# Decode attention with a 16,384-long cache: the weighted sum of V with V as the moving operand in four column groups

## The chip, the cores and the metric

One core of a Trainium2 chip. The metric is device time in microseconds (us), lower is better. A program of one core has no second die to compare with; runs count as undisturbed ("fast") by the rule that a run must lie within 1.5% of the fastest of its kernel.

## The reference, cut to what matters

```python
# B, H, Sk, Dh, D = 2, 32, 16384, 128, 1024; bf16 throughout
def _A_ref(x, k_cache, v_cache, wq, wo):              # attention of one new token
    q = (x @ wq).reshape(B, 1, H, Dh).transpose(0, 2, 1, 3)
    scores = einsum("bhqd,bhkd->bhqk", q, k_cache) * Dh ** -0.5
    p = softmax(scores)
    o = einsum("bhqk,bhkd->bhqd", p, v_cache)         # <- the change is here
    return o.transpose(0, 2, 1, 3).reshape(B, 1, H * Dh) @ wo
# ... _B_ref: a small mixer block on its own weights (about 18.9 MB)
out = g * _A_ref(...) + (1 - g) * _B_ref(...)         # g: a sigmoid gate
```

There are 64 pairs of batch and head. Each has 4 MB of K and 4 MB of V, read once and used for one query. All loads together are 572.5 MB.

## The kernel before

K and V tiles share a ring of five 4 MB buffers (128 partitions x 32 KB). One queue (SP) issues all the big loads, in the order K of pair i+1, V of pair i, and each load waits for the buffer used five loads earlier. Partition p holds rows 128p to 128p+127 of the cache; `V[:, j, :]` is the 128 x 128 slice of row j of every partition.

```python
NM = 8; CJ = NJ // NM                       # NJ = 128 rows per partition, CJ = 16
def qk_stage(i):                            # scores of a pair
    for m in range(NM):
        nc.vector.transpose(out=T..., in_=Kw[:, m * CW : (m + 1) * CW]...)   # 32x32 blocks
        for v in range(4):
            nc.tensor.matmul(S[:], lhsT=z[:, v, 7 - m : 7 - m + P],
                             rhs=Tb[:, v // 2, :, v % 2], start=..., stop=...)   # 512 columns
# softmax_stage: max, exp on ACT, PT = the exponentials, transposed in 32x32 blocks
def pv_stage(i):                            # weighted sum of V
    tot_ps = misc_psum([P, 1], FP32)
    nc.tensor.matmul(tot_ps[:], lhsT=quarter_f[:], rhs=rs[:], start=True, stop=True)
    nc.vector.reciprocal(out=rinv[:], in_=tot_ps[:])
    oc = ops.tile([P, 1], FP32, name="oc")
    for j in range(NJ):                     # 128 weight loads of V, 128 one-column matmuls
        nc.tensor.matmul(oc[:], lhsT=V[:, j, :], rhs=PT[:, j % CJ, j // CJ : j // CJ + 1],
                         start=(j == 0), stop=(j == NJ - 1))
    nc.vector.tensor_scalar(out=OT[:, h, b : b + 1], in0=oc[:], scalar1=rinv[:, 0:1], ...)
# [cut: q projection, gate, mixer, output projection]
```

## Time and profile before

| | before |
|---|---|
| time, median | 1355.92 us |
| span of the profiled run | 1353.7 us, 24,547 instructions |
| DMA share, 40 to 1280 us | 1.00, at 429 GB/s |
| PE busy | 971.3 us (72%) |
| weighted sum of a pair on PE | 3.3 to 3.5 us, 256 instructions |

The page of the kernel before: instructions, busy times, then the DMA queues (packets, MB, share of the time of 16 DMA engines). q1 is the queue of the loads; q8 and q14 bring instructions.

```profile
span 1353.7 us, 24547 instructions
PE 971.3 (72%) x11260; PEld 525.9 (39%) x11260; DVE 752.0 (56%) x948; ACT 51.7 (4%) x132; POOL 34.0 (3%) x79
...
q1 hardware_dynamic: 24628, 572.54, 98.8%
q8 instruction: 88, 1.44, 0.4%
q14 instruction: 15, 0.12, 0.0%
```

The table by stretches (us, busy time of each engine, PE clock, DMA share, GB/s) of the same kernel, for the middle:

```profile
40.00:600.00 560.00, 417.36 (x4680) 228.13 (x4679) 319.37 (x402) 21.38 (x56) 13.51 (x28) 0.72 1.00 429
600.00:1280.00 680.00, 488.32 (x5541) 257.31 (x5539) 382.09 (x467) 25.69 (x66) 16.26 (x34) 0.74 1.00 429
```

```profile
1326.00:1330.00 4.00, 0.65 (x2) 0.25 (x3) 1.95 (x2) 0.00 (x0) 0.00 (x0) 0.50 0.99 418
1333.00:1337.00 4.00, 4.00 (x15) 1.54 (x14) 3.54 (x4) 0.00 (x0) 0.00 (x0) 0.79 0.55 236
1342.00:1346.00 4.00, 4.00 (x141) 4.00 (x139) 1.10 (x3) 0.15 (x2) 0.00 (x0) 0.50 0.52 211
```

In the middle all 16 DMA engines are busy all the time. From 1333 to 1346 us only 0.55, then 0.52 of the DMA engines' time is used. If every load is dealt out evenly over the 16 engines, as its 128 packets of 32 KB suggest (8 for each engine), some engines have fallen behind during the run.

Two groups of the kernel before (line, engine, operation, out<-in, count, busy us, mean ns, then idle time just before and what ended it):

```profile
L247 DVE STREAM_TRANSPOSE T<-Kn 128x1024 f32<-128x1024 f32 x512 | 597.0, 1217 | 202.7 <-DMA Kn<-in_A_k_cache_dram 174.7
...
L296 PE MATMUL oc<-PT,Vn 128*128 128x1 bf16 x8192 | 221.5, 164 | 0.7 <-issue 0.7
```

The vector engine waits 174.7 us for K: compute has slack. The weighted sum is the second line.

### The profile page before, as it was taken

The page shows a single profiled execution, that of the slowest core. Times are in us where ns is not written, and L with a number is a line of the kernel's source. Part 1 is how long each engine was busy: PE and PEld are TensorE (multiplying, and loading weights), DVE is VectorE, ACT ScalarE, POOL GpSimd, SP SyncE. Part 2 cuts the span into 40 slices and gives each one's busy share as a digit, 9 for nine tenths or more (in the row PEclk, how much of TensorE's full clock was granted, in tenths as well). Part 3 has the DMA queues.
Part 4 walks back from the last instruction along what each step waited for, and adds up shares of the span by engine and source line. Part 5 has one row for each costly group of instructions (what it writes and reads, how often), then busy time and mean ns, then how long its engine had stood idle before and what let it go on. Part 6 is the DMA issues. An engine that isn't in the chain of part 4 may idle for free.

```text
span 1353.7 us, 24547 instructions
## 1 busy us (share of the span) xinstructions
PE 971.3 (72%) x11260; PEld 525.9 (39%) x11260; DVE 752.0 (56%) x948; ACT 51.7 (4%) x132; POOL 34.0 (3%) x79
## 2 busy tenths in 40 slices
PE   2787677787777777677676767767766776776767
PEld 2343343344444344343433334334333333333434
DVE  2766555565545654556545555655655664665564
ACT  0000000000000000000000000000000000000000
POOL 0000000000000000000000000000000000000000
PEclk9887676766767766777676868777767777867876
DMA  9999999999999999999999999999999999999995
GB/s 403 431 434 425 429 431 428 430 430 428 430 429 428 430 429 430 432 427 428 431 430 428 431 427 433 426 430 433 427 428 431 426 434 430 427 427 431 427 433 242
DMA packets 25011, 574.11 MB, mean 424 GB/s; under 512 B 3014, under 2 KB 3014, under 8 KB 7372
## 3 DMA queue, kind: packets, MB, share of 16 engines
q1 hardware_dynamic: 24628, 572.54, 98.8%
q8 instruction: 88, 1.44, 0.4%
q14 instruction: 15, 0.12, 0.0%
q10 hardware_dynamic: 280, 0.01, 0.0%
HBM read 572.53 MB, written 0.00 MB: 423 GB/s over the span
## 4 chain that ended last, share of the span: by engine, by line
DMA 70%; PE 20%; DVE 6%; issue 2%; ACT 1%; DVEq 0%; POOL 0%; ACTq 0%
DMA Kn<-in_A_k_cache_dram 69%; PE S L255 12%; PE oc L296 5%; DVE T L247 5%; DMA x_pm<-in_A_x_dram 2%; DVE m L266 1%; PE misc L400 1%; PE misc L272 1%; PE misc L199 1%; ACT Pr L277 1%; PE misc L373 1%; DVE mx L270 0%; PE misc L268 0%; PE misc L291 0%; DVE nb L274 0%
## 5 line engine op out<-in xcount | busy, mean ns | idle before, releaser
L247 DVE STREAM_TRANSPOSE T<-Kn 128x1024 f32<-128x1024 f32 x512 | 597.0, 1217 | 202.7 <-DMA Kn<-in_A_k_cache_dram 174.7
L255 PE MATMUL S<-T,z_131 128*128 128x512 bf16 x704 | 211.0, 464 | 82.3 <-DVE T L247 81.8
L255 PE MATMUL S<-T,z_135 128*128 128x512 bf16 x672 | 201.5, 464 | 83.9 <-DVE T L247 83.5
L255 PE MATMUL S<-T,z_133 128*128 128x512 bf16 x672 | 201.3, 463 | 75.7 <-DVE T L247 75.2
L296 PE MATMUL oc<-PT,Vn 128*128 128x1 bf16 x8192 | 221.5, 164 | 0.7 <-issue 0.7
L296 PEld LDWEIGHTS <-Vn 128*128 128x128 bf16 x8192 | 220.8, 100 | 1.4 <-issue 0.8
L255 PEld LDWEIGHTS <-z_131 128*128 128x128 bf16 x704 | 79.0, 112 | 215.0 <-issue 162.5
L255 PEld LDWEIGHTS <-z_135 128*128 128x128 bf16 x672 | 75.1, 112 | 210.3 <-issue 160.7
L255 PEld LDWEIGHTS <-z_133 128*128 128x128 bf16 x672 | 75.3, 112 | 201.6 <-issue 152.0
L303 DVE TENSOR_SCALAR OT<-oc,rinv 128x1 bf16<-128x1 f32 x64 | 14.2, 221 | 150.6 <-PE oc L296 150.6
L277 ACT ACTIVATE Pr<-S,nb 128x512 bf16<-128x512 f32 x64 | 44.0, 687 | 1236.4 <-DVE nb L274 1211.8
L266 DVE TENSOR_REDUCE m<-S 128x1 f32<-128x512 f32 x64 | 44.3, 692 | 76.2 <-PE S L255 76.2
L281 DVE STREAM_TRANSPOSE PT<-Pr 128x512 bf16<-128x512 bf16 x64 | 45.5, 711 | 56.4 <-ACT Pr L277 56.4
L291 PE MATMUL misc<-rs,quarter_f 128*128 128x1 f32 x128 | 31.9, 318 | 35.8 <-ACT Pr L277 35.8
L268 PE MATMUL misc<-ident_f,m 128*1 128x128 f32 x64 | 17.7, 276 | 45.4 <-DVE m L266 45.4
L272 PE MATMUL misc<-mx,nscale_f 1*128 1x1 f32 x128 | 25.0, 262 | 24.6 <-DVE mx L270 24.6
L291 PEld LDWEIGHTS misc<-rs,quarter_f 128*128 128x128 f32 x128 | 27.1, 264 | 38.6 <-ACT Pr L277 38.6
L268 PEld LDWEIGHTS misc<-ident_f,m 128*1 128x1 f32 x64 | 5.2, 81 | 76.1 <-DVE m L266 75.2
L272 PEld LDWEIGHTS misc<-mx,nscale_f 1*128 1x128 f32 x128 | 19.5, 190 | 37.3 <-DVE mx L270 37.3
L270 DVE TENSOR_REDUCE mx<-misc 1x1 f32<-1x128 f32 x64 | 17.8, 278 | 26.8 <-PE misc L268 26.6
L274 DVE COPY nb<-misc 128x1 f32<-128x1 f32 x64 | 10.0, 157 | 30.0 <-PE misc L272 30.0
L225 POOL TENSOR_TENSOR z_131<-qsel,own 128x64 bf16<-128x64 bf16 x22 | 10.5, 477 | 429.5 <-PE S L255 423.0
(77 smaller groups left out, 184.4 us busy)
## 6 DMA issues: line engine op xcount, KB each, us to landing
Kn<-in_A_k_cache_dram SPq DMA_DIRECT2D x64, 4096.0 KB, 42.7
Vn<-in_A_v_cache_dram SPq DMA_DIRECT2D x63, 4096.0 KB, 39.9
wt<-in_B_w_dram SPq DMA_DIRECT2D x4, 3584.0 KB
woh<-in_A_wo_dram SPq DMA_DIRECT2D x32, 256.0 KB, 39.7
wq_156<-in_A_wq_dram SPq DMA_DIRECT2D x1, 4096.0 KB, 12.2
wq_158<-in_A_wq_dram SPq DMA_DIRECT2D x1, 4096.0 KB, 21.7
wt<-in_B_w_dram SPq DMA_DIRECT2D x2, 2048.0 KB
Vn<-in_A_v_cache_dram SPq DMA_DIRECT2D x1, 2048.0 KB
```

The source lines that it names most:

```text
L199: nc.tensor.matmul(qps[:, h, :], lhsT=wq_half[half][:, r, h * Dh : (h + 1) * Dh], rhs=xT[:, half * rn + r, :], start=(r == 0), stop=(r == ...
L247: nc.vector.transpose(out=T[:].rearrange("p w j s -> p j w s"), in_=Kw[:, m * CW : (m + 1) * CW].rearrange("p (j w e) -> p j w e", w=2, e=32),
L255: nc.tensor.matmul(S[:], lhsT=z[:, v, 7 - m : 7 - m + P], rhs=Tb[:, v // 2, :, v % 2], start=(m == 0 and v == 0), stop=(m == NM - 1 and v ...
L266: nc.vector.reduce_max(out=m[:], in_=S[:], axis=AX.X)
L268: nc.tensor.transpose(mT[:], m[:], ident_f[:])
L270: nc.vector.reduce_max(out=mx[:], in_=mT[:], axis=AX.X)
L272: nc.tensor.matmul(nb_ps[:], lhsT=nscale_f[:], rhs=mx[:], start=True, stop=True)
L277: nc.scalar.activation(out=Pr[:], in_=S[:], func=ACTF.Exp, bias=nb[:], scale=scale, accum_out=rs[:])
L281: nc.vector.transpose(out=PT[:].rearrange("p j m -> p (j m)"), in_=Pr[:])
L291: nc.tensor.matmul(tot_ps[:], lhsT=quarter_f[:], rhs=rs[:], start=True, stop=True)
L296: nc.tensor.matmul(oc[:], lhsT=V[:, j, :], rhs=PT[:, j % CJ, j // CJ : j // CJ + 1], start=(j == 0), stop=(j == NJ - 1),)
L303: nc.vector.tensor_scalar(out=OT[:, h, b : b + 1], in0=oc[:], scalar1=rinv[:, 0:1], scalar2=None, op0=ALU.mult)
```

## The change

Its intent: V becomes the moving operand. One matmul streams four rows of V (512 columns) past 32 columns of weights, and four such matmuls, in four 32-column groups of the PE array, are to run side by side. That leaves a 128 x 512 block of which only some rows of some columns matter; it is copied out of PSUM and four products with a constant selection matrix pick and sum them. The last pair keeps the old form, as its V arrives last and the new form has a longer way from the last byte to the result.

```diff
+    osel = const.tile([P, 4], FP32)
+    nc.vector.tensor_copy(out=osel[:], in_=ident_f[:, 0:8:2])
+    for g in range(1, 4):
+        nc.vector.tensor_tensor(
+            out=osel[:], in0=osel[:], in1=ident_f[:, 40 * g : 40 * g + 8 : 2], op=ALU.add)
...
+    def pv_rows(V, PT, oc):
+        O = ops.tile([P, 4 * Dh], FP32, name="O")
+        for m in range(NM):
+            lhsT = PT[:].rearrange("p j m -> p (j m)")[:, m : CJ * 32 : 16]
+            for g in range(4):
+                j0 = m * CJ + 4 * g
+                nc.tensor.matmul(O[32 * g : 32 * g + 32, :], lhsT=lhsT, rhs=V[:, j0 : j0 + 4, :],
+                                 start=(m == 0), stop=(m == NM - 1))
+        Os = rows.tile([P, 4, Dh], FP32, name="Os")
+        nc.scalar.copy(out=Os[:].rearrange("p x d -> p (x d)"), in_=O[:])
+        for x in range(4):
+            nc.tensor.matmul(oc[:], lhsT=Os[:, x, :], rhs=osel[:, x : x + 1],
+                             start=(x == 0), stop=(x == 3))
+    def pv_cols(V, PT, oc):                 # the old loop
...
-        oc = ops.tile([P, 1], FP32, name="oc")
-        for j in range(NJ): ...
+        oc = misc_psum([P, 1], FP32)
+        (pv_rows if i < NPAIR - 1 else pv_cols)(V, PT, oc)
```

To free a PSUM bank, the result column moves into three shared PSUM buffers, and the last product of the mixer no longer holds two of these between its halves: each half is summed and added by itself (cut here).

More of the change, by code (lines that the diff above doesn't have):

```diff
@@ L157 @@
         nc.vector.memset(own[32 * a : 32 * a + 32, 4 * a : 4 * a + 4], 1.0)
+    assert CJ == 16
+    osel = const.tile([P, 4], FP32)
+    nc.vector.tensor_copy(out=osel[:], in_=ident_f[:, 0:8:2])
+    for g in range(1, 4):
+        nc.vector.tensor_tensor(
+            out=osel[:], in0=osel[:], in1=ident_f[:, 40 * g : 40 * g + 8 : 2], op=ALU.add
+        )
     ZW = P + 8
@@ L283, in softmax_stage @@
         rs_tiles[i] = rs
+    def pv_rows(V, PT, oc):
[4 more added lines that the diff above has]
+                j0 = m * CJ + 4 * g
+                nc.tensor.matmul(
+                    O[32 * g : 32 * g + 32, :],
+                    lhsT=lhsT,
+                    rhs=V[:, j0 : j0 + 4, :],
+                    start=(m == 0),
+                    stop=(m == NM - 1),
+                )
+        Os = rows.tile([P, 4, Dh], FP32, name="Os")
+        nc.scalar.copy(out=Os[:].rearrange("p x d -> p (x d)"), in_=O[:])
+        for x in range(4):
+            nc.tensor.matmul(
+                oc[:], lhsT=Os[:, x, :], rhs=osel[:, x : x + 1], start=(x == 0), stop=(x == 3)
+            )
+    def pv_cols(V, PT, oc):
+        for j in range(NJ):
+            nc.tensor.matmul(
+                oc[:],
+                lhsT=V[:, j, :],
+                rhs=PT[:, j % CJ, j // CJ : j // CJ + 1],
+                start=(j == 0),
+                stop=(j == NJ - 1),
+            )
     def pv_stage(i):
@@ L293, in pv_stage @@
         nc.vector.reciprocal(out=rinv[:], in_=tot_ps[:])
-        oc = ops.tile([P, 1], FP32, name="oc")
-        for j in range(NJ):
-            nc.tensor.matmul(
-                oc[:],
-                lhsT=V[:, j, :],
-                rhs=PT[:, j % CJ, j // CJ : j // CJ + 1],
-                start=(j == 0),
-                stop=(j == NJ - 1),
-            )
+        oc = misc_psum([P, 1], FP32)
+        (pv_rows if i < NPAIR - 1 else pv_cols)(V, PT, oc)
         nc.vector.tensor_scalar(
@@ L394 @@
     wt = {}
-    b_ps = []
     def linear_rows(w, actT, r0, rn, dst, first, last):
@@ L439, in st_lin4 @@
     def st_lin4(half):
-        if half == 0:
-            b_ps.extend(misc_psum([B, W], FP32) for _ in range(DH2))
-        linear_rows(wt.pop(f"w4{half}"), h2T, half * (FC // 2), FC // 2, b_ps, half == 0, half == 1)
+        ps = [misc_psum([B, W], FP32) for _ in range(DH2)]
+        linear_rows(wt.pop(f"w4{half}"), h2T, half * (FC // 2), FC // 2, ps, True, True)
+        for n in range(DH2):
+            sl = slice(n * W, (n + 1) * W)
+            nc.vector.tensor_tensor(
+                out=pre_row[:, sl], in0=(x1_row if half == 0 else pre_row)[:, sl], in1=ps[n][:], op=ALU.add
+            )
         if half == 1:
-            for n in range(DH2):
-                sl = slice(n * W, (n + 1) * W)
-                nc.vector.tensor_tensor(out=pre_row[:, sl], in0=x1_row[:, sl], in1=b_ps[n][:], op=ALU.add)
             nc.vector.tensor_scalar(
```

## The prediction

> **What bounds it now.** The loads. The queue table gives the SP queue 98.8% of the time of 16 DMA engines over a 1353.7 us span (572.5 MB, mean 424 GB/s). The table by stretches shows a DMA share of 1.00 at 429 GB/s from 40 to 1280 us: the transfers never wait for a buffer. The ring of five 4 MB tiles is refilled 40 to 43 us ahead (issue table, time to landing). The chain of waits is 70% DMA. The Trainium skill ("DMA: Bandwidth & Descriptors", Specifications) gives a fabric ceiling of 435 GB/s; the trace's 429 agrees that little is left.
>
> A pair of K and V (8.39 MB) takes 19.6 us at 429 GB/s. Compute has slack: in the list of waits the vector engine waits for K 174.7 us in 60 times (2.9 us a pair).
>
> **What the change does,** per pair, for 63 of 64:
> - Removes 128 one-column matmuls with 128 weight loads of V: 3.3 to 3.5 us in the timeline, 27 ns each (221.5 us in all).
> - Adds 32 matmuls of 512 columns. In the trace a 512-column score matmul follows the last by 0.43 us at the low clock, 0.22 at the high. Estimates: four column groups side by side, 8 x 0.22 to 0.43 = 1.8 to 3.4 us; one after another, 7 us (14 at the low clock). The skill ("TensorE: Matmul & The Clock Gate", Packing small matmuls) reports 2.38x for three column tiles; I expect about 3x for four: 2.3 to 4.6 us.
> - Adds a 128x512 ACT copy, about 0.69 us (as the 128x512 exponential), and four fp32 selection matmuls, 0.3 to 0.5 us each by the fp32 sum with `quarter_f` (two passes, 0.38 to 0.57 us): 1.2 to 2 us, plus about 1 us of handoffs.
>
> So a pair's weighted sum goes from 3.5 us to about 5 (4 to 8). The added 1.5 us fits in the 2.9 us of slack and the 30 us of prefetch. Little of the change lies on the critical path.
>
> Two small terms remain. The instruction queue moved 1.44 MB; with some 11,000 of 24,547 instructions fewer 0.65 MB goes, 1.5 us at 429 GB/s (an estimate). At the end the last V lands at about 1348.3 us and 5 us of work follow, unchanged; the pair before it is off that path by about 0.7 us, so its selection may add 0 to 1 us.
>
> **Predicted: 1354.8 us, 8 in 10 between 1352.0 and 1362.0. Faster by over 2%: 1%; within 2%: 93%; slower by over 2%: 6%.**
>
> **What would show each step right.** DMA share still 1.00 at 428 to 431 GB/s in the middle; instruction bytes near 0.8 MB; the 32 matmuls of a pair done in 2 to 4.6 us; the vector engine's wait for K shorter by about 1.5 us a pair, yet not zero; chain still led by the K loads; last V landing within 3 us of before.
>
> **What would make it wrong.** If the column groups run one after another, the stage takes 7 us at the high clock plus 3 for copy and selection: 6 us over, more than the slack; then K waits for compute, DMA share drops under 0.97 and the time is 1380 to 1480. Waits might also come from the single buffers of the new tiles, or the 3 shared PSUM buffers that now also hold the result column. If the transfers share something with PE's reads of V, the rate in the middle would change (430 to 433 GB/s would give 5 to 10 us); I expect no change. Faster by 2% would need a rate above 437 GB/s.

## The result, and the profile after

The time fell from 1355.92 us (four runs, 1355.86 to 1356.09) to 1347.86 us (four runs, 1347.82 to 1348.12). The ratio is 0.9941, 95% interval 0.9924 to 0.9958. Ratios are the mean time of one kernel's fast runs over that of the other's of the same rounds, so not quite the ratio of the medians. The change is within 2%, as forecast, but 8.1 us is more than the range allowed: it lies below its lower end of 1352.

The page after, in the same order:

```profile
span 1346.0 us, 13528 instructions
PE 955.1 (71%) x5716; PEld 452.2 (34%) x5716; DVE 743.6 (55%) x954; ACT 88.4 (7%) x195; POOL 34.4 (3%) x79
...
q1 hardware_dynamic: 24628, 572.54, 99.3%
q8 instruction: 44, 0.72, 0.2%
q14 instruction: 15, 0.12, 0.0%
```

The stretches after, middle and end (1338 to 1340 us in place of 1326 to 1330, as the end comes sooner):

```profile
40.00:600.00 560.00, 411.04 (x2429) 197.33 (x2427) 315.65 (x403) 36.61 (x83) 14.13 (x29) 0.75 1.00 430
600.00:1280.00 680.00, 485.06 (x2644) 222.16 (x2645) 378.99 (x472) 46.18 (x102) 16.05 (x33) 0.76 1.00 430
```

```profile
1333.00:1337.00 4.00, 2.04 (x19) 1.40 (x11) 0.57 (x3) 1.20 (x3) 0.00 (x0) 0.84 0.56 232
1338.00:1340.00 2.00, 2.00 (x77) 2.00 (x77) 0.01 (x1) 0.00 (x0) 0.00 (x0) 0.50 0.38 143
1342.00:1346.00 4.00, 0.84 (x2) 0.00 (x0) 1.40 (x2) 0.00 (x0) 0.00 (x0) 0.50 0.00 1
```

PE busy time hardly moved, and the bytes loaded are the same. What halved is the q8 queue: 88 packets of 16 KB became 44. And the lopsided end is shorter: nine engines still work at 1333 us as before, but at 1342 the loads are over, where before eight engines had 5 us to go.

The new stage in the timeline of a pair (start us, length us):

```profile
1312.70 1.96 PE L302 MATMUL O<-Vn,PT 128*32 128x512 bf16 x32
...
1314.77 0.58 ACT L310 COPY Os<-O 128x512 f32<-128x512 f32 x1 [16.64 <-PE O L302]
...
1315.40 1.05 PE L312 MATMUL misc<-osel,Os 128*128 128x1 f32 x8 [0.74 <-ACT Os L310]
```

All 32 matmuls take 1.96 us, the copy 0.58, the selection 1.05: with the handoffs 3.8 us, against 3.5. Single records show four matmuls starting 2 to 5 ns after one another, and the next four 207 ns after the last of them: the four groups do run side by side. The Trainium skill ("TensorE: Matmul & The Clock Gate", Packing small matmuls) gives about 4 ns per tile; this trace agrees.

And the vector engine's wait for K:

```profile
L255 DVE STREAM_TRANSPOSE T<-Kn 128x1024 f32<-128x1024 f32 x512 | 596.1, 1216 | 114.7 <-DMA Kn<-in_A_k_cache_dram 89.9
```

It fell from 174.7 to 89.9 us, 1.3 us a pair. That is the loss of slack that was forecast, and the DMA share of 1.00 in the middle shows that it is harmless.

One more thing changes, at the very end. The last pair's K, and after the change its products with V (128 weight loads and matmuls, as before), in the timelines before and after:

```profile
1328.05 4.62 DVE L247 STREAM_TRANSPOSE T<-Kn 128x1024 f32<-128x1024 f32 x4 [2.81 <-DMA Kn<-in_A_k_cache_dram]
```

```profile
1337.96 3.55 PE L318 MATMUL misc<-PT,Vn 128*128 128x1 bf16 x128 [0.16 <-DVE PT L289]
```

Before, the vector engine starts on the last K at 1328.05 us, after at 1320.86: also 7.2 us sooner. Before, PE stands still for 0.73 us before the last 29 of the products, about when the last piece of V lands. After, the products run without a gap, so there the path to the end leads from the landing of the last K and not from the last V. Both landings wait for the engines that are late.

### When each DMA engine ends

The trace does not number the engines, but its packet records let one see when an engine runs dry: a packet end that no packet start follows within 60 ns, where each start is counted for one end only. Worked out so, to within some tenths of a microsecond, the last load packets end at:

```
                q8 packets   early group        one between   late group
before          88           7, 1330.8-1332.1   1340.5        8, 1347.4-1347.7
after           44           7, 1330.6-1332.2   } 1338.6-1338.8 and 1340.0-1340.5, about half each
```

So eight engines are 16 us late before, and 7 to 9 us late after. 88 packets over 8 engines are 11 each; 44 are 5.5, that is 5 on some and 6 on others, and the late group has indeed split in two, 1.5 us apart. 11 x 1.46 = 16.1 us, 6 x 1.46 = 8.8, 5 x 1.46 = 7.3. The factor 1.46 is this lag divided by these counts. Packet times give nearly the same: an instruction packet itself takes 1.07 us (mean of 88), and the load packet right behind it some 1.7 us in place of 1.22: about 1.5 us for both.

**Theory.** PE's instructions are fetched over 8 of the 16 DMA engines, 256 at a time (22,520 in 88 packets). Each fetch makes its engine about 1.5 us late with the loads. The engines share each load evenly, so the engine with the most fetches sets when the last loads, of K and of V, are complete. The change halves PE's instructions and with them this lag; that V moves is not what counts.

**Rivals.** (a) Reading V as weights took something from the transfers into the same memory. (b) The new stage frees buffers sooner, or does better work on PE. (c) One of the side parts (PSUM, mixer) did it.

### The profile page after: what moved, and what is told of

Its sections match the earlier page's. It is cut to its first block, busy times and chain, and to the rows that moved or that the text cites. A ratio compares the mean times of both kernels' runs of the same rounds, so it can differ in the third digit from the quotient of the medians.

```text
span 1346.0 us, 13528 instructions
## 1 busy us (share of the span) xinstructions
PE 955.1 (71%) x5716; PEld 452.2 (34%) x5716; DVE 743.6 (55%) x954; ACT 88.4 (7%) x195; POOL 34.4 (3%) x79
## 4 chain that ended last, share of the span: by engine, by line
DMA 61%; PE 26%; DVE 8%; issue 2%; ACT 1%; DVEq 0%; POOL 0%; ACTq 0%
DMA Kn<-in_A_k_cache_dram 37%; DMA Vn<-in_A_v_cache_dram 22%; PE S L263 14%; DVE T L255 6%; PE O L302 5%; PE misc L433 2%; DMA x_pm<-in_A_x_dram 2%; PE misc L312 2%; PE misc L407 1%; ACT Pr L285 1%; DVE PT L289 1%; ACT Os L310 1%; PE misc L207 1%; PE misc L280 0%; PE misc L318 0%
## 5 line engine op out<-in xcount | busy, mean ns | idle before, releaser
L255 DVE STREAM_TRANSPOSE T<-Kn 128x1024 f32<-128x1024 f32 x512 | 596.1, 1216 | 114.7 <-DMA Kn<-in_A_k_cache_dram 89.9
L302 PE MATMUL O<-Vn,PT 128*32 128x512 bf16 x2016 | 133.3, 410 | 40.0 <-DMA Vn<-in_A_v_cache_dram 40.0
L337 DVE TENSOR_SCALAR OT<-misc,rinv 128x1 bf16<-128x1 f32 x64 | 14.1, 221 | 246.1 <-PE misc L312 242.6
L263 PEld LDWEIGHTS <-z_136 128*128 128x128 bf16 x704 | 81.7, 116 | 180.3 <-issue 125.7
L263 PEld LDWEIGHTS <-z_138 128*128 128x128 bf16 x672 | 78.7, 117 | 183.5 <-issue 132.7
L263 PEld LDWEIGHTS <-z_140 128*128 128x128 bf16 x672 | 79.3, 118 | 176.4 <-issue 126.4
L302 PEld LDWEIGHTS <-PT 128*32 128x32 bf16 x2016 | 69.9, 143 | 100.5 <-DMA Vn<-in_A_v_cache_dram 48.0
L312 PE MATMUL misc<-osel,Os 128*128 128x1 f32 x504 | 69.6, 259 | 47.2 <-ACT Os L310 47.2
L310 ACT COPY Os<-O 128x512 f32<-128x512 f32 x63 | 36.9, 585 | 994.5 <-PE O L302 994.5
L312 PEld LDWEIGHTS misc<-osel,Os 128*128 128x128 f32 x504 | 64.2, 200 | 78.4 <-ACT Os L310 78.4
L332 PE MATMUL misc<-rs,quarter_f 128*128 128x1 f32 x128 | 35.8, 349 | 67.0 <-ACT Pr L285 67.0
L332 PEld LDWEIGHTS misc<-rs,quarter_f 128*128 128x128 f32 x128 | 30.7, 297 | 72.7 <-ACT Pr L285 72.3
## 6 DMA issues: line engine op xcount, KB each, us to landing
Kn<-in_A_k_cache_dram SPq DMA_DIRECT2D x64, 4096.0 KB, 46.1
```

The costliest lines, as they stand in the source:

```text
L255: nc.vector.transpose(out=T[:].rearrange("p w j s -> p j w s"), in_=Kw[:, m * CW : (m + 1) * CW].rearrange("p (j w e) -> p j w e", w=2, e=32),
L263: nc.tensor.matmul(S[:], lhsT=z[:, v, 7 - m : 7 - m + P], rhs=Tb[:, v // 2, :, v % 2], start=(m == 0 and v == 0), stop=(m == NM - 1 and v ...
L302: nc.tensor.matmul(O[32 * g : 32 * g + 32, :], lhsT=lhsT, rhs=V[:, j0 : j0 + 4, :], start=(m == 0), stop=(m == NM - 1),)
L310: nc.scalar.copy(out=Os[:].rearrange("p x d -> p (x d)"), in_=O[:])
L312: nc.tensor.matmul(oc[:], lhsT=Os[:, x, :], rhs=osel[:, x : x + 1], start=(x == 0), stop=(x == 3))
```

## The experiments

All runs: correct against the reference unless said, beside the kernel before on the same chip (1355.95 to 1356.06 us). A caution: a kernel that was wrong passed the comparison too (`const` below), so "correct" says little about the weighted sum here.

### ctrl: everything but the moving V

```diff
-        (pv_rows if i < NPAIR - 1 else pv_cols)(V, PT, oc)
+        pv_cols(V, PT, oc)
```

> The changed kernel with V stationary for all 64 pairs; every other part of the change stays (selection constant, result column in the shared PSUM buffers, the last product of the mixer summed in two parts). Fetch theory (instruction fetches ride on 8 of the 16 DMA engines, delay their loads by about 1.5 us each, and the slowest engine sets the end): the instruction count is back at about 24,500, so 88 instruction packets and 1356 us (1354.5 to 1357.5). If the side parts made the gain: 1348.

Measured: 1355.34 us (1354.59 to 1356.04), ratio 0.9995 (0.998 to 1.001), 88 instruction packets, late engines at about 1347.8 (one at 1346.1). Rival (c) falls: the side parts give about half a microsecond.

### const: the same instructions, V not read as weights

```diff
-                lhsT=V[:, j, :],
+                lhsT=V[:, 0, :] if j == 0 else ident_bf[:],
```

> The kernel before with the same 128 weight loads and matmuls a pair, but 127 of the 128 weight loads read the constant identity in place of V (wrong result on purpose; the first still reads V, so that the buffer is held until then). Fetch theory: same instructions, so 88 packets and 1355.9 us, within 1 us. Rival (reading V into the array as weights takes something from the transfers that write the same memory): with these reads gone the time falls to 1350 or below, the rate in the middle rises.

Measured: 1355.90 us (1355.64 to 1356.30), ratio 1.000, 88 packets, late engines at 1347.4 to 1347.6 but for one that ends sooner, the middle still at 429 GB/s. Rival (a) falls: 127 of 128 reads of V less, and nothing gained.

### pad_pe and pad_pool: two pads that did not test what they should

```diff
 # pad_pe, in pv_stage
+        for _ in range(96 if i < NPAIR - 1 else 0):
+            nc.tensor.ldweights(ident_bf[:, 0:32])
 # pad_pool, in build_z
+        for _ in range(192):
+            nc.gpsimd.nop(nofuse=True)
```

> The changed kernel plus 96 weight loads of a constant (32 columns) a pair on PE, 6,048 instructions in all, without any other work. Fetch theory: 24 instruction packets more (44 to 68), 24 / 8 x 1.45 us = 4.3 us later: 1352.2 us (1350.5 to 1354), and the two groups of DMA engines finish about 12.5 us apart instead of 8. Rivals (reads of V, or buffers freed sooner): 1347.9, unless the 1 to 3 us of PE time a pair make compute the bound; that would show as a DMA share under 1.00 in the middle.

> The changed kernel plus 192 empty instructions a pair on POOL, about 12,300 in all, where nothing waits for them. Fetch theory, if fetches of every engine use the same DMA engines: 48 packets more (44 to 92), 48 / 8 x 1.45 = 8.7 us later: 1356.6 us (1354 to 1359). If POOL's fetches use other DMA engines than PE's, they load the early ones and the time stays near 1348 to 1350. Rivals: 1347.9 in any case, since PE, V and the buffers are as in the changed kernel.

Measured: pad_pe 1483.50 us (1482.92 to 1484.33). The constant depends on no pair, so all 6,048 weight loads were scheduled to the front, where the loads stood still for some 130 us (2 GB/s in three slices of the page). It had 68 instruction packets, but the late engines end at 1474.2 to 1476.1 against 1466.4 to 1468.0 for the early: 8 us apart as with 44. The 24 extra packets were fetched at the front (the pad runs from 1.5 us to about 180), most of them while the load queue was idle. That fits the theory (a fetch costs only where it displaces a load), though it was not the test.

pad_pool: 1347.85 us (1347.63 to 1348.95), 44 packets, no instruction more in the trace. The empty instructions left no mark on either instruction queue, so the run says nothing about the theory. Both pads missed what was expected of them (1352.2 and 1356.6 us).

### pad48 and pad96: the change with PE instructions given back

The pads now read the pair's own weights, so they stay in their place:

```diff
+        for _ in range(48 if i < NPAIR - 1 else 0):      # pad96: 96
+            nc.tensor.ldweights(PT[:, 0, :])
         oc = misc_psum([P, 1], FP32)
```

> The changed kernel plus 48 idle weight loads (of the pair's own weights, so that they stay in their place) a pair on PE: 3,024 instructions, 12 packets more, 56 in all. Fetch theory in its sharper form (the packets go round 8 DMA engines, each delays its engine by 1.46 us, the engine with most of them ends last): 7 on each in place of 5 or 6, so the last load lands 1.5 us later, at about 1341.7, and the time is 1349.3 us (1348.3 to 1350.3). Rivals (V as weights; PE work in itself): 1347.9, or later only with a DMA share under 1.00 in the middle.

> The same with 96: 6,048 instructions, 68 packets. Fetch theory: 8 or 9 on each of 8 engines, the last load lands at 1331.5 + 9 x 1.46 = 1344.6, 4.4 us later than in the changed kernel: 1352.2 us (1351 to 1353.5), if compute with 2 us more of PE a pair still keeps up (DMA share 1.00 in the middle). Rivals: 1347.9.

Measured: pad48 1349.08 us (1348.66 to 1349.29), pad96 1352.38 us (1352.02 to 1352.81), against 1349.3 and 1352.2 expected. The queue lines of both pages, pad48 first:

```profile
q8 instruction: 56, 0.92, 0.3%
```

```profile
q8 instruction: 68, 1.11, 0.3%
```

The late engines end at 1341.7 to 1341.9 in pad48 (56 packets, 7 each: the group is one again), and in pad96 (68, or 8.5 each) in two groups, 1343.0 to 1343.2 and 1344.8 to 1344.9. The stretches of pad96, middle and end:

```profile
600.00:1280.00 680.00, 482.19 (x2691) 304.62 (x5857) 384.00 (x474) 45.62 (x100) 16.58 (x34) 0.78 1.00 430
```

```profile
1338.00:1340.00 2.00, 1.33 (x10) 1.13 (x10) 0.41 (x2) 0.24 (x1) 0.00 (x0) 0.93 0.53 223
1342.00:1346.00 4.00, 3.63 (x129) 3.48 (x128) 0.46 (x3) 0.00 (x0) 0.00 (x0) 0.50 0.23 89
```

The middle is untouched (share 1.00), so compute keeps up and only the end moves. Over all runs with even flow (not `pad_pe`, `g_outer` and the two `rebal` runs, whose loads stood still or slowed down) the end of a late engine against its number of packets is:

```
packets on the engine    5        6        7        8        9        11
last load ends, us       1338.7   1340.3   1341.8   1343.1   1344.8   1347.6
```

(1347.6 - 1338.7) / 6 = 1.48 us a packet. This is the test that rival (b) fails: V moves and PE does the same useful work as in the changed kernel, yet 4.5 of the 8.1 us are gone again with half of the instructions (6,048 of 11,019). The eight engines are worked out from ends; no record names them.

### pad_pool2: instructions of another engine

One engine ends between the two groups in every run. I guessed that it carries the other instruction queue, q14.

```diff
         z = z_tiles[i % NZ]
+        for _ in range(32):
+            nc.gpsimd.memset(z[:, 0, 0:1], 0.0)
```

> The changed kernel plus 32 one-element clears of a zero a pair on POOL (tied to the pair's z tile, so that they stay in their place), 2,048 instructions that nothing waits for. One DMA engine ends between the early seven and the late eight in every run (at 1340.5 in the kernel before); the theory says that it carries the other instruction queue, 8 KB a packet for all engines but PE. If so, 16 packets more on that one engine, some 0.56 us each (9 us of lag for the 16 of now): it ends at about 1349.5 and the time is 1357 us (1354 to 1359), from a sixth of the instructions that the change removed. If POOL's fetches ride on the eight like PE's: 8 packets, 1349.3. If they cost nothing: 1347.9.

Measured: 1350.30 us (1349.94 to 1350.56); the time was expected at 1357. The queue line of its page:

```profile
q14 instruction: 31, 0.25, 0.0%
```

The packets came as expected: 15 became 31, 8 KB for 128 instructions. But they did not add up on the engine that I named. Only six engines now end early, and the last of all ends at 1342.6 in place of 1340.5. So at least some packets of POOL fell on an engine that had been early; which of the late ends is that engine, the trace does not tell. Shown is that another engine's instructions cost time as well: 2,048 on POOL cost 2.4 us, more than 3,024 on PE (1.2 us). That they are spread over fewer than eight engines would explain it, and fits the one early engine that is gone, but is not shown further. My guess of a single engine for all of q14 was wrong.

### rebal3 and rebal6_before: shifting loads from late to early engines

```diff
+        if i in (20, 36, 52):                    # rebal6_before: six V tiles
+            for p0, p1 in ((0, 112), (112, 120), (120, 128)):
+                nc.sync.dma_start(out=tv[p0:p1], in_=src[p0:p1])
+            vn_tiles[i] = t
+            return
```

> The changed kernel, but three of the V tiles are loaded as 112 partitions (7 rows for each of 16 engines) and twice 8 partitions[...]: 8 engines get 3 rows of 32 KB more in sum than the mean, 8 get 3 fewer, 1.22 us each. Fetch theory: if the 8 engines that get more are the early ones, the late ones end 3.7 us sooner: 1344.2 us (1343 to 1346); if they are the late ones, 3.7 us later: 1351.5. Rivals (rate or compute bound, engines alike): 1347.9 within 1.

> The kernel before with six V tiles loaded that way and nothing else changed, all 24,500 instructions and V stationary kept. Fetch theory: the late engines are 16 us behind seven of the others; 6 rows x 1.22 us moved from the late to the early make 1355.9 - 7.3 = 1348.6 us (1347 to 1350.5), the gain of the change without the change; if the engines favoured are the late ones, 1363. Rivals: 1355.9.

Measured: rebal3 1414.60 us (1410.81 to 1421.84), rebal6_before 1541.40 us (1534.31 to 1548.85). Both far off every expectation. Stretches of rebal3 before, within and after one of its three tiles:

```profile
440.00:450.00 10.00, 8.77 (x31) 3.36 (x31) 9.14 (x8) 0.00 (x0) 0.00 (x0) 0.75 1.00 430
460.00:470.00 10.00, 5.43 (x16) 1.95 (x16) 6.37 (x6) 0.00 (x0) 0.00 (x0) 0.55 1.03 223
473.00:480.00 7.00, 1.12 (x5) 0.29 (x3) 0.69 (x1) 0.00 (x0) 0.48 (x1) 0.94 1.14 159
495.00:505.00 10.00, 4.22 (x12) 1.94 (x13) 5.75 (x9) 0.78 (x2) 0.00 (x0) 0.56 1.00 428
```

The engines are all busy, but at half and then a third of the rate: a 32 KB packet takes 2.4, then 3.8 us (means of the two stretches) in place of 1.22. The Trainium skill ("DMA: Bandwidth & Descriptors", Specifications) has 16 engines on 16 ports of the on-chip memory, by convention 8 partitions an engine. If the 112 partitions go 7 to an engine, the engines no longer keep to sets of 8, and a load of 8 partitions may put several engines on one set. Engines getting in each other's way at a port would look like this; no run isolates it, and on how many engines a load of 8 partitions runs, which the expectations took for granted, no trace shows. So it stays an explanation that was only argued. As a test of the theory the pair is void, and as a remedy it fails. A busy DMA share at a fallen rate is worth remembering: the share alone does not show it.

### fewer: fewer PE instructions still

Three small fp32 products become bf16; each of these is four instructions in the trace in fp32 (two weight loads, two matmuls), and two in bf16.

```diff
-    quarter_f = const.tile([P, P], FP32)   # likewise nscale_f, osel, mx, rs and Os
+    quarter_f = const.tile([P, P], BF16)
```

> The changed kernel with the selection products, the bias of the exponential and the normaliser in bf16 in place of fp32 (half as many PE instructions each): 760 fewer, 41 packets in place of 44, and about 1 us less of PE a pair. Fetch theory with the slowest engine setting the end: seven of the eight engines now have 5 packets, one 6, and the engine of the other queue still ends at about 1340.4: nothing gained, 1347.9 us (1347.3 to 1348.2). If the mean over the engines counted: 1347.3 or less. If PE time counted: 1346 or below.

Measured: 1347.36 us (1347.23 to 1347.62), 41 packets. The loads end at 1340.7, no sooner than after the change (1340.5), though the late engines are now at 1338.4 to 1338.9: the engine between the groups is the last, as far as ends tell engines apart. The 0.5 us come from the end: the last pair's softmax is shorter, its products start at 1337.05 in place of 1337.96 us and wait for the last piece of V again. It is the fastest kernel, by half a microsecond, at a price in precision that the comparison would not show. As expected, cutting more of PE's instructions alone buys next to nothing now, while PE busy time fell from 955.1 to 842.9 us. Some 20 us of this are records that are missing: 64 of the 2,048 score matmuls have none in `fewer`, and `pad_pool`, the changed kernel with the same gap, shows 935.0.

### rows_last: is V stationary for the last pair worth it?

```diff
-        (pv_rows if i < NPAIR - 1 else pv_cols)(V, PT, oc)
+        pv_rows(V, PT, oc)
```

> The changed kernel with V moving for the last pair too. The loads end as before; after the last piece of V the copy out of PSUM (0.6 us) and the selection (1.05 us) with their handoffs stand on the path in place of the last of the one-column matmuls: 0.5 to 2 us later, 1348.4 to 1349.9 us. This is what keeping V stationary for the last pair is worth.

Measured: 1350.17 us (1350.14 to 1350.86), 2.3 us slower than the change, a little beyond the range. After the last piece of V, in the timeline:

```profile
1340.72 0.65 PE L302 MATMUL O<-Vn,PT 128*32 128x512 bf16 x4 [0.54 <-DMA Vn<-in_A_v_cache_dram]
...
1341.47 0.59 ACT L310 COPY Os<-O 128x512 f32<-128x512 f32 x1 [4.40 <-PE O L302]
...
1342.11 1.86 PE L312 MATMUL misc<-osel,Os 128*128 128x1 f32 x8 [0.74 <-ACT Os L310]
```

The selection takes 1.86 us here, not the 1.05 of the middle. The exception for the last pair earns its place: without it over a quarter of the gain is lost.

### g_outer: the column groups one after another

```diff
-        for m in range(NM):
-            lhsT = ...
-            for g in range(4):
+        for g in range(4):
+            for m in range(NM):
+                lhsT = ...
```

> The changed kernel with its two loops exchanged: the eight matmuls of one column group follow each other, so that neighbours are never in different groups except at three places. Same instructions, same packets. If matmuls overlap only when neighbours are in different column groups, the 32 take 32 x 0.22 = 7 us in place of 1.96, 5 us more a pair than the slack of about 2 us allows: compute becomes the bound, the DMA share in the middle falls under 1.00, and the time is 1400 to 1560 us. If the array overlaps them anyway, 1347.9.

Measured: 1376.80 us (1375.51 to 1378.27), ratio 1.0154 (1.0139 to 1.0169). Slower, but less than expected. A stage of its timeline:

```profile
613.41 4.72 PE L302 MATMUL O<-Vn,PT 128*32 128x512 bf16 x32
```

The stage takes 4.72 us in place of 1.96, not the 7 expected: in the records some starts are 215 ns apart, but others 6 or 61 ns. The matmuls may not have been issued in the order of my loops; the trace does not name a matmul's column group, so this stays open. A pair now takes 20.2 us (613.41 to 633.65), more than the 19.6 of its loads. Yet the DMA share in the middle stayed at 1.00 and the last load ended at 1340.8. The loads ran ahead of compute as long as buffers allowed: the median time from issue of a K load to its landing fell from 46.1 to 29.2 us, and the lag of compute came out at the end as some 30 us without loads. In this run a slight compute bound was hidden by the ring and then paid in one piece.

## Why the prediction was right or wrong

**Right: what bounds the kernel, and that PE work was not it.** The DMA share in the middle stayed at 1.00 (429, then 430 GB/s). PE busy time went from 971 to 955 us and the time did not follow it. In `fewer` PE busy time fell by about 90 us for half a microsecond. The chain that ended last is still led by the K loads, though less so: 37% of the span, with 22% for V, against 69% for K before.

**Right: the stage.** Estimated 1.8 to 3.4 us side by side, with the skill's factor 2.3 to 4.6; measured 1.96. Copy 0.69, measured 0.58; selection 1.2 to 2, measured 1.05. The whole took 3.8 us, a little under the forecast of 4 to 8, as the handoffs took about 0.2 us and not 1. Slack lost: 1.5 us a pair forecast, 1.3 measured. This agreement is partly luck: the stage is only 0.3 us longer than before, not 1.5, and where the rest of the slack went was not traced (PE now waits for V, 40.0 us in 7 places). Instruction bytes near 0.8 MB: 0.72.

**Wrong: the instruction fetches.** The step that failed is, as the prediction put it, "with some 11,000 of 24,547 instructions fewer 0.65 MB goes, 1.5 us at 429 GB/s". The mechanism was named and its size was off by a factor of about five. Three things were missing from that term:

1. The packets do not spread over 16 engines but over eight (late group of eight in every run with even flow): twice as much per engine.
2. A 16 KB packet costs its engine about 1.48 us, where 16 KB at 429 GB/s over 16 engines take 0.61 us (an estimate from the rate): 2.4 times as much.
3. The slowest engine decides, not the mean. By the mean over 16 engines the q8 packets' own time fell by only 5.88 - 2.95 = 2.9 us.

44 packets less, 16 KB each, at 429 GB/s are 1.7 us; times 2 times 2.4 are 8. In the engines' terms: 11 packets became at most 6, and the last load ended at 1340.5 in place of 1347.7. That is 7.2 of the 7.8 us between the two profiled spans. The other 0.6 us lie after the last load (4.9 us from it to the end of the output's transfer before, 4.3 after): the products of the last pair no longer stand still for V (0.73 us before). The last K came 7.2 us sooner as well (1320.86 in place of 1328.05), and after the change it is this landing that leads to the end. So "last V landing within 3 us of before" was wrong as well.

**What I could have seen.** The end of the trace before: a DMA share of 0.55 and 0.52 over more than 10 us, with loads outstanding. I read the mean share of the middle and the 0.4% of the instruction queue, and took both for averages that were alike on every engine.

**Open.** Which engines the eight are; which engines carry q14; what made the split loads slow; the issue order in `g_outer`. None of these bears on where the 8 us came from.

## What to carry to other kernels

When loads bound a kernel, look at how its transfers end: here a DMA share that fell to about a half for over 10 us meant that some engines were behind, and what delayed these (PE's own instruction stream) was on the critical path though its mean share was 0.4%. Many tiny instructions then have a price besides engine time; replacing 256 of them a pair by about 80 paid off although the engine was hardly less busy, and further cuts stopped paying where another engine became the last. An extra instruction used as a probe should be tied to data of its place: in `pad_pe` the scheduler carried it elsewhere.

## What the Trainium skill lacked or had wrong

- "Runtime: NRT & Kernel Launch", Instruction fetch mechanics, describes the fetches: blocks of 16 KiB, 256 instructions, each brought by a DMA. The trace agrees (88 packets of 16 KB for PE's 22,520 instructions). The section calls their cost mostly hidden. Where the loads are the bound it was not hidden here: about 1.48 us of delay on the engine that carries a packet, so that 88 packets made eight engines 16 us late. No page says that PE's packets fall on 8 of the 16 engines.
- "DMA: Bandwidth & Descriptors", Queues, rings and completion order, says that an engine takes turns between queue rows packet by packet. The traces agree: a 16 KB instruction packet (1.07 us) sits between two load packets. It lacks what this costs a load.
- The same section puts refills on row 14, as runtime-internal. Here queue 14 did bring instructions (15 packets became 31 of 8 KB with 2,048 instructions on POOL, and the kernel became 2.4 us slower), but PE's came on queue 8, if the trace's queue numbers are the page's rows (44 became 56 and 68 with the pads on PE, while queue 14 stayed at 15).
- The same page, Specifications, gives 8 partitions an engine as a convention. No page gives the price of a load split against it beside full loads: three V tiles split as 112 + 8 + 8 partitions cost 66.7 us (1414.60 against 1347.86), with packets of 2.4 to 3.8 us in place of 1.22.
- "TensorE: Matmul & The Clock Gate", Packing small matmuls, measured three column tiles at 2.38x and has no figure for four. Four took 1.96 us for 32 matmuls of 512 columns, with 207 ns from the last of one set of four to the first of the next.
